# A state-space and gated-MLP block on one core: the recurrence tile laid out by residue, correction products written in contiguous runs, and a new order of stages

## The chip, the core and the metric

The kernel runs on one NeuronCore of a Trainium2 chip. The metric is the time of one execution on the device in microseconds (us); lower is better. The profile's span, first to last instruction, is 2 to 3 us shorter than this time (351.6 of 353.73 us before). TensorE is called PE in the profile, its weight load PEld, VectorE DVE, ScalarE ACT, GpSimd POOL, and SP issues the DMAs. "Busy" is the time in which something of an engine, or of a group of instructions, was running. Where one instruction follows another on an engine, the two overlap in the trace (products before: 1.42 us long, 1.13 from start to start); "busy" counts such time once, while the mean duration of one instruction contains it in full. So busy times of groups that alternate cannot be added, and for cost I use the distance from start to start and say so.

## The reference

```
x = A_x                                   # 2048 tokens x 640, bf16
xn = layernorm(x)
# A: a diagonal complex recurrence with 640 states
h[t] = Lam_bar * h[t-1] + (B_bar @ xn[t])
yA   = 2 * Re(C @ h[t]) + Dskip * xn[t]
# B: a gated MLP with mixing over tokens
z  = gelu(xn @ w_in);  z1 = z[:, :864];  z2 = layernorm(z[:, 864:])
g  = w_sp @ z2 + b_sp                     # 2048 x 2048 times 2048 x 864
yB = (z1 * g) @ w_out
out = x + yA + yB
```

## The kernel before

A small scheduler inside the kernel lists all operations with guessed costs, simulates the engines and fixes one order of instructions for each queue. TensorE's order is the program's own. All queues then run strictly in that order, and a wait at the head holds up what stands behind it (in the DMA queue once for 17.4 us, as shown below).

Time is split into 256 blocks of eight tokens; the token of residue j is the j-th of its block. The recurrence is done in three parts: inside each block (`horner`, seven steps from residue to residue), over the 256 block ends (`scan`), and a correction that adds the block's incoming state to each residue (`fix`). The tile of states keeps four residues interleaved, so that one residue is a row of 2-byte elements four apart:

```python
def lj(q, j):                 # q: which 128 of the 640 states
    return lv(q, j // 4).rearrange("p (x j) -> p x j", j=4)[:, :, j % 4]

def horner(q, j, half):       # 70 steps of 3; (r, m) = (re/im, 128 blocks)
    ...
    scalar_tensor_tensor(tv, prev, lr, cur, mult, add)                    # L648, 256 wide, float32 out
    scalar_tensor_tensor(dst[:, 0], prev[:, 1], nli, tv[:, 0], mult, add) # L650, 128 wide, bf16 out
    scalar_tensor_tensor(dst[:, 1], prev[:, 0], li,  tv[:, 1], mult, add) # L652, 128 wide, bf16 out

def fix(q, jg):
    pv = [m.ap(2048).rearrange("p (r n j) -> p r n j", r=2, j=4) for m in (P, Q)]
    for jj in range(n):       # n = 4 or 3 residues
        activation(pv[0][:, :, :, jj], hv[:, 1:3, 1:257], Identity, scale=a)  # L707, planned at ca(512, ptr=1) = 0.615 us
        activation(pv[1][:, :, :, jj], hv[:, 0:2, 1:257], Identity, scale=b)  # L709
    lq += P;  lq += Q         # L713, 2048 wide, all four residues at once
# an output tile of residue j waits for l_iv(q, j // 4): all four residues of its group

z2_tiles(0, 8)
for q in range(5):            # state inputs and recurrence, first half of the tokens
    bu(q, 0, 0); bu(q, 1, 0); horner(q, 1..7, 0)
z2_tiles(8, 16)
... kappa(); t_comb(0, 2, 4, 6)          # sums of z2 for the spatial product (L853)
for q in range(5):            # the same for the second half, then the scan
    bu(q, 0, 1); bu(q, 1, 1); horner(q, 1..7, 1); scan(q)
... z1 tiles, stored to DRAM; c_scaled()
for j in range(8): s_comb(j); spatial(j); ...   # 7 products instead of 8; sums of W on VectorE (L874)
outputs
```

## Time and profile before

| | before |
|---|---|
| time, median | 354.48 us (352.74 to 355.24, 3 runs); 354.86 us with a fourth |
| profiled span | 351.6 us |
| TensorE busy / waiting | 290.2 us / 58.2 us (sum of the waits below) |
| mean granted clock | 0.913 |
| VectorE, ScalarE busy | 247.8 us, 207.4 us |

The page's second part shows 40 slices of 8.8 us; a digit is the busy share in tenths, PEclk the granted clock.

```profile
PE   7799999999999505999896563497397699999996
...
DVE  4868999999999999999894542355655333345442
ACT  2899999964545201236979999999999221000000
...
PEclk9899999999999955999999686678879699999999
```

Slices are counted from 0. VectorE is full from slice 4 to 18 (35 to 167 us; the scans end at 158), ScalarE from slice 21 to 30 (185 to 272 us), and TensorE has holes beside both. Only the last quarter is TensorE's alone.

What TensorE waited for, in total, by the waits:

```profile
PE ps L917 <- ACT arena L930: 28.9, 9, 5.6
PE ps L917 <- ACT arena L602: 16.3, 1, 16.3
PE ps L999 <- DVE arena L1016: 8.3, 2, 5.5
PE ps L532 <- DVE arena L518: 3.0, 1, 3.0
PE ps L463 <- POOL arena L459: 1.3, 1, 1.3
PE ps L917 <- DVE arena L874: 0.4, 1, 0.4
```

The columns are total us, number and longest. The spatial products (L917) waited 28.9 us for evictions on ScalarE (L930) and once 16.3 us for z1's gelu (L602), which itself waited for a store. Groups of instructions, shapes kept apart (busy us, mean ns of one, then idle time before):

```profile
L707 ACT ACTIVATE arena<-arena 128x512 bf16<-128x512 bf16 x35 | 49.7, 1421 | 1.5 <-DVE arena L839 1.0 <-DVE arena L713 0.3
L709 ACT ACTIVATE arena<-arena 128x512 bf16<-128x512 bf16 x35 | 49.4, 1412 | 0.1
L648 DVE SCALAR_TENSOR_TENSOR arena<-arena 128x256 f32<-128x256 bf16 x70 | 31.4, 478 | 0.3
L650 DVE SCALAR_TENSOR_TENSOR arena<-arena 128x128 bf16<-128x128 bf16 x60 | 27.0, 508 | 0.0
L713 DVE TENSOR_TENSOR arena<-arena 128x2048 bf16<-128x2048 bf16 x20 | 24.5, 1224 | 41.0 <-ACT arena L707 28.2 <-ACT arena L709 12.8
```

A product (L707, L709) lasts 1.4 us for 512 elements, while the squares of 864 contiguous elements on the same engine (L573) last 0.94 us. The DMA queue's timeline before the 16.3 us pause (start, us issuing, what):

```profile
98.95 14.19 SPq L353 DMA_DIRECT2D z_scratch<-arena  x12
130.51 1.24 SPq L351 DMA_TRANSPOSE arena<-in_B_w_sp_dram  x1
131.80 1.05 SPq L353 DMA_DIRECT2D z_scratch<-arena  x2
```

From 113 to 130.5 us nothing is issued: a load of W stands at the head, and two stores of z1 behind it.

### The profile page before, as it was taken

The numbers are of one execution on the slowest core, as the hardware profiler recorded it, in microseconds if no ns is written. First come the engines' busy times: TensorE is split into PE (matmuls) and PEld (weight loads), VectorE is DVE, ScalarE is ACT, GpSimd is POOL, SyncE is SP. The second block draws the span as 40 slices with busy tenths as digits, with TensorE's granted clock in tenths as the row PEclk, the third lists the DMA queues.
The fourth block names the chain that finished last, engine by engine and source line by source line (L and its number), as shares of the span: only waits on it lengthen the run. The fifth ranks groups of instructions, "written<-read, shape, count | busy, mean of one in ns | idle before, by whom it ended". The sixth has DMA issues, their size and how long they took to land.

```text
span 351.6 us, 4404 instructions
## 1 busy us (share of the span) xinstructions
PE 290.2 (83%) x1587; PEld 169.8 (48%) x1587; DVE 247.8 (70%) x611; ACT 207.4 (59%) x270; POOL 26.7 (8%) x50
## 2 busy tenths in 40 slices
PE   7799999999999505999896563497397699999996
PEld 3454445544777402545443221154144357777774
DVE  4868999999999999999894542355655333345442
ACT  2899999964545201236979999999999221000000
POOL 3439320011000000000000000000000000000000
PEclk9899999999999955999999686678879699999999
DMA  7968463000054008577969391057422030552211
GB/s 245 229 145 220 90 89 62 2 0 0 2 171 150 3 0 241 120 147 122 191 132 209 95 202 37 0 106 111 103 66 74 23 82 2 108 129 75 76 56 37
DMA packets 81186, 34.73 MB, mean 99 GB/s; under 512 B 68526, under 2 KB 81166, under 8 KB 81166
## 3 DMA queue, kind: packets, MB, share of 16 engines
q1 hardware_dynamic: 81022, 34.39, 43.1%
q8 instruction: 12, 0.20, 0.2%
q14 instruction: 8, 0.07, 0.1%
q10 hardware_dynamic: 144, 0.08, 0.1%
HBM read 12.29 MB, written 6.18 MB: 53 GB/s over the span
## 4 chain that ended last, share of the span: by engine, by line
DVE 36%; PE 30%; ACT 28%; POOL 3%; issue 2%; DVEq 0%; POOLq 0%
ACT arena L707 12%; ACT arena L709 12%; PE ps L999 11%; DVE arena L648 7%; DVE arena L650 7%; PE ps L917 7%; PE ps L1007 7%; DVE arena L652 6%; DVE arena L668 4%; PE ps L559 3%; DVE arena L853 2%; POOL arena L749 2%; PE ps L463 2%; DVE arena L590 1%; ACT arena L930 1%
## 5 line engine op out<-in xcount | busy, mean ns | idle before, releaser
L917 PE MATMUL ps<-arena 128*128 128x432 bf16 x448 | 96.6, 381 | 45.6 <-ACT arena L930 28.9
L917 PEld LDWEIGHTS ps<-arena 128*128 128x128 bf16 x448 | 46.5, 106 | 94.8 <-ACT arena L930 33.0
L559 PE MATMUL ps<-arena 128*128 128x432 bf16 x320 | 61.4, 351 | 0.0
L999 PE MATMUL ps<-arena 128*128 128x320 bf16 x320 | 51.0, 319 | 8.3 <-DVE arena L1016 8.3
L713 DVE TENSOR_TENSOR arena<-arena 128x2048 bf16<-128x2048 bf16 x20 | 24.5, 1224 | 41.0 <-ACT arena L707 28.2
L707 ACT ACTIVATE arena<-arena 128x512 bf16<-128x512 bf16 x35 | 49.7, 1421 | 1.5 <-DVE arena L839 1.0
L709 ACT ACTIVATE arena<-arena 128x512 bf16<-128x512 bf16 x35 | 49.4, 1412 | 0.1
L559 PEld LDWEIGHTS ps<-arena 128*128 128x128 bf16 x320 | 38.7, 122 | 19.0 <-issue 1.5
L999 PEld LDWEIGHTS ps<-arena 128*128 128x128 bf16 x320 | 37.6, 118 | 20.3 <-DVE arena L1016 9.0
L617 PE MATMUL ps<-arena 128*128 128x512 bf16 x200 | 45.3, 386 | 0.0
L930 ACT ACTIVATE arena<-ps,arena 128x432 f32<-128x432 f32 (+1 forms) x32 | 19.7, 618 | 28.1 <-PE ps L917 28.1
L1007 PE MATMUL ps<-arena 128*128 128x320 bf16 (+1 forms) x224 | 33.1, 299 | 0.0
L602 ACT ACTIVATE arena<-ps 128x864 bf16<-128x864 f32 x16 | 14.0, 891 | 30.4 <-DMA z_scratch<-arena 21.6
L648 DVE SCALAR_TENSOR_TENSOR arena<-arena 128x256 f32<-128x256 bf16 x70 | 31.4, 478 | 0.3
L617 PEld LDWEIGHTS ps<-arena 128*128 128x128 bf16 x200 | 19.2, 96 | 25.7
L650 DVE SCALAR_TENSOR_TENSOR arena<-arena 128x128 bf16<-128x128 bf16 (+1 forms) x70 | 29.9, 485 | 0.0
L652 DVE SCALAR_TENSOR_TENSOR arena<-arena 128x128 bf16<-128x128 bf16 (+1 forms) x70 | 29.6, 483 | 0.2
L1016 DVE TENSOR_TENSOR arena<-ps,arena 128x640 bf16<-128x640 f32 x15 | 12.3, 823 | 23.3 <-PE ps L1007 23.3
L1007 PEld LDWEIGHTS ps<-arena 128*128 128x128 bf16 (+1 forms) x224 | 21.9, 98 | 8.3
L623 ACT CAST arena<-ps 128x1024 bf16<-128x1024 f32 x20 | 20.1, 1014 | 9.8 <-PE ps L617 9.6
L874 DVE TENSOR_TENSOR arena<-arena 128x1024 bf16<-128x1024 bf16 x32 | 22.1, 692 | 1.6 <-PE ps L917 1.6
L668 DVE TENSOR_TENSOR arena<-arena 128x512 f32<-128x512 f32 (+2 forms) x40 | 22.2, 577 | 0.0
(87 smaller groups left out, 251.1 us busy)
## 6 DMA issues: line engine op xcount, KB each, us to landing
arena<-in_A_x_dram SPq DMA_DIRECT2D x32, 160.0 KB, 3.2
z_scratch<-arena SPq DMA_DIRECT2D x16, 216.0 KB, 2.0
arena<-z_scratch SPq DMA_DIRECT2D x8, 432.0 KB, 4.7
out_dram<-arena SPq DMA_DIRECT2D x15, 160.0 KB, 2.0
arena<-in_B_w_in_dram SPq DMA_DIRECT2D x10, 216.0 KB, 3.9
arena<-in_B_w_out_dram SPq DMA_DIRECT2D x1, 960.0 KB, 6.3
arena<-in_B_w_sp_dram SPq DMA_TRANSPOSE x32, 4.0
arena<-arena SPq DMA_TRANSPOSE x20, 2.9
```

What stands on the lines that cost most here:

```text
L559: r = e.matmul(ps[:, b + h, 0:FG], lhs(k), winv[:, k, hcol * FH + h * FG:hcol * FH + (h + 1) * FG], start=(k == 0), stop=(k == ND - 1))
L617: r = e.matmul(ps[:, b + ri, :], btv[:, ri, k, q * 128:(q + 1) * 128], rhs[k], start=(k == 0), stop=(k == ND - 1))
L648: dve(lambda e: e.scalar_tensor_tensor(tv, prev, lr, cur, op0=ALU.mult, op1=ALU.add), rd + cr, [t.iv()], cd(256), nm + "a")
L650: dve(lambda e: e.scalar_tensor_tensor(dst[:, 0], prev[:, 1], nli, tv[:, 0], op0=ALU.mult, op1=ALU.add), rd + cr + [t.iv(0, 512)], dw[0:1] ...
L652: dve(lambda e: e.scalar_tensor_tensor(dst[:, 1], prev[:, 0], li, tv[:, 1], op0=ALU.mult, op1=ALU.add), rd + cr + [t.iv(512, 512)], dw[1:2 ...
L668: tt = lambda o, a, b, op: (lambda e: e.tensor_tensor(o, a, b, op))
L707: act(lambda e, a=a, jj=jj: e.activation(pv[0][:, :, :, jj], hv[:, 1:3, 1:257], ACT.Identity, scale=a), [h.iv(), Civ("a")], [P.iv()], ca(5 ...
L709: act(lambda e, b=b, jj=jj: e.activation(pv[1][:, :, :, jj], hv[:, 0:2, 1:257], ACT.Identity, scale=b), [h.iv(), Civ("b")], [Q.iv()], ca(5 ...
L713: dve(lambda e, m=m: e.tensor_tensor(lq, lq, m.ap(2048), ALU.add), [l_iv(q, jg), m.iv()], [l_iv(q, jg)], cd(2048, 2), "fix%s%d%d" % (nm, q ...
L917: r = e.matmul(ps[:, bk, 0:FG], lv_[:, k, :], rv[k], start=(first and k == 0), stop=(k == 7), skip_group_check=True)
L999: r = e.matmul(ps[:, b + n, 0:320], hv[:, o:o + 128], cpv[:, ri, q, n * 320:(n + 1) * 320], start=(q == 0 and ri == 0), stop=False, skip_g ...
L1007: r = e.matmul(ps[:, b + n, 0:320], gv[0:kk, k, :], wov[0:kk, k, n * 320:(n + 1) * 320], start=False, stop=(k == 6), skip_group_check=True)
```

## The change

The intent is that every write of 2-byte elements be contiguous. The state tile becomes residue-major, so a recurrence step takes all 256 blocks at once in half as many instructions; the copies from PSUM take the residues apart; products get small contiguous tiles of their own; corrections are done residue by residue, just ahead of the outputs. Around that: all z2 tiles come first, loads and warm-up at the start are reordered, fewer layernorm tiles go to ScalarE, and a pointer scalar costs 0.06 us more in the plan. (Gate products 864 wide, sums of W on VectorE and the output base from strided rows of x stand in both kernels; the diff does not touch them.)

```diff
 def lj(q, j):
-    return lv(q, j // 4).rearrange("p (x j) -> p x j", j=4)[:, :, j % 4]
+    return l_m.ap(512, BF16, (q * 8 + j) * 1024)
 # bu: state inputs out of PSUM
-act(lambda e: e.copy(o, ps[:, b:b + 2, :]), ...)                     # 1024 wide
+for ri in range(2):
+    act(lambda e, ri=ri: e.copy(o[:, ri, :, half, :], ps[:, b + ri, :].rearrange("p (m j) -> p j m", j=4)), ...)
 # horner: the same three instructions, 512, 256 and 256 wide, once per (q, j); two q interleaved
-def horner(q, j, half):
+def horner(q, j):
 # fix
-def fix(q, jg):   # 4 residues, products interleaved, 2 adds of 2048
+def fix(j):       # all five q of one residue
+    for q in range(5):
+        for lo, sc in ((1, a), (0, b)):
+            pv = m.ap(512).rearrange("p (r n) -> p r n", r=2)        # m: ring of 8 contiguous tiles
+            activation(pv, hv[:, lo:lo + 2, 1:257], Identity, scale=sc)
+            tensor_tensor(lq, lq, m.ap(512), add)
+                                                                 # (cut: residue 7, one copy for each q)
 # outputs
-pe(mmh, [l_iv(q, j // 4) for q in range(5)] + ...)
+pe(mmh, [l_iv(q, j) for q in range(5)] + ...)
 # order of stages
-z2_tiles(0, 8); <bu, horner of half 0>; z2_tiles(8, 16); <bu, horner of half 1, scan>
+z2 tiles 0..15, each before the next transpose; then per q: bu (both halves), t_comb, horner of two q, scan
+# start: loads "x0 w0 x1 w1 w2 x2 w3 w4 x3 x4 x5", gelu table loaded at once, 11 warm-up matmuls for 14
-ACT_LN = (3, 5, 7, 9, 11, 13, 15)
+ACT_LN = (3, 6, 9, 12)
+PTR = 0.06        # added to planned costs of instructions with a pointer scalar
 ... (sines grouped under one table load, scaled C computed in place)
```

More of the change, by code (lines that the diff above doesn't have):

```diff
@@ L279, in bass_parallel_sum__ssm_conv_s5__mixer_gmlp__prompt_kernel @@
         rt = r2.sub(14336)
-        ht_m = [rt.sub(1024) for _ in range(4)]
+        ht_m = [rt.sub(2048) for _ in range(2)]
         sc_m = [rt.sub(2048) for _ in range(3)]
-        s8_m = [rt.sub(2048) for _ in range(2)] + s_m[3:6]
-        e3 = Mem(wa_m.lo, 16384 + 3 * 2048)
+        s8_m = [rt.sub(2048) for _ in range(2)] + s_m[5:6]
+        e3 = Mem(wa_m.lo, 16384 + 5 * 2048)
         x_m = [e3.sub(1280) for _ in range(11)]
@@ L290, in bass_parallel_sum__ssm_conv_s5__mixer_gmlp__prompt_kernel @@
         q1 = r1.again()
-        pq_m = [q1.sub(4096) for _ in range(2)]
+        pq_m = [q1.sub(1024) for _ in range(8)]
         cf_m = [q1.sub(1728) for _ in range(5)]
@@ L375, in win_iv, with l_iv @@
             return win_m.iv((k * 2 + h) * FH * 2, FH * 2)
-        def l_iv(q, jg, ri=None, half=None):
+        def l_iv(q, j, ri=None, half=None):
+            o = (q * 8 + j) * 1024
             if ri is None:
-                return l_m.iv((q * 2 + jg) * 4096, 4096)
-            return l_m.iv((((q * 2 + jg) * 2 + ri) * 2 + half) * 1024, 1024)
-        def lv(q, jg):
-            return l_m.ap(2048, BF16, (q * 2 + jg) * 4096)
+                return l_m.iv(o, 1024)
+            return l_m.iv(o + ri * 512 + half * 256, 256)
         def lj(q, j):
-            return lv(q, j // 4).rearrange("p (x j) -> p x j", j=4)[:, :, j % 4]
+            return l_m.ap(512, BF16, (q * 8 + j) * 1024)
         cpos = {}
@@ L434, in bass_parallel_sum__ssm_conv_s5__mixer_gmlp__prompt_kernel @@
         FIRST = []
-        load_x(0, bias=5000)
-        load_win(0, 1, "sp", bias=4900)
-        load_x(1, bias=4800)
-        for k in range(1, ND):
-            load_win(k, 1, "sp", bias=4800 - 10 * k)
-        for i in range(2, 6):
-            load_x(i, bias=4700 - 10 * i)
+        for n, w in enumerate("x0 w0 x1 w1 w2 x2 w3 w4 x3 x4 x5".split()):
+            if w[0] == "x":
+                load_x(int(w[1]), bias=5000 - 20 * n)
+            else:
+                load_win(int(w[1]), 1, "sp", bias=5000 - 20 * n)
         for n, a in enumerate((A_Lambda_re, A_Lambda_im, A_log_dt)):
@@ L460, in bass_parallel_sum__ssm_conv_s5__mixer_gmlp__prompt_kernel @@
         pool(lambda e: e.memset(C("e"), math.e), [], [Civ("e")], 0.2, "e")
-        NW = 14
+        act(lambda e: e.activation(zero_m.ap(8, BF16, 1024), zero_m.ap(8), ACT.Gelu_apprx_tanh), [zero_m.iv(0, 1024)],
+            [zero_m.iv(1024, 16)], 1.4, "gelu table", bias=9000)
+        NW = 11
         for n in range(NW):
@@ L518, in ln_x @@
             dve(lambda e: e.tensor_scalar(xn.ap(D), x, mu, rstd, op0=ALU.subtract, op1=ALU.mult),
-                [xm.iv(), ri, mi if i in ACT_LN else siv(i, 12, 13)], [xn.iv()], cd(D, 4), "xn%d" % i)
+                [xm.iv(), ri, mi if i in ACT_LN else siv(i, 12, 13)], [xn.iv()], cd(D, 4) + 2 * PTR, "xn%d" % i)
         def xn_T(i):
@@ L591, in z2_norm @@
                                                         op0=ALU.subtract, op1=ALU.mult),
-                    [z2iv(i), s2iv(2, i, i + 1), s2iv(6, i, i + 1)], [z2iv(i)], cd(FH, 4), "z2n%d" % i)
+                    [z2iv(i), s2iv(2, i, i + 1), s2iv(6, i, i + 1)], [z2iv(i)], cd(FH, 4) + 2 * PTR, "z2n%d" % i)
         nz1 = [0]
@@ L621, in bu @@
                "bu%d%d%d" % (q, jg, half))
-            o = lv(q, jg).rearrange("p (r h x) -> p r h x", r=2, h=2)[:, :, half, :]
-            act(lambda e: e.copy(o, ps[:, b:b + 2, :]), [bank(b), bank(b + 1)],
-                [l_iv(q, jg, 0, half), l_iv(q, jg, 1, half)], ca(1024, psum=True), "u%d%d%d" % (q, jg, half))
+            o = l_m.ap(2048, BF16, (q * 8 + jg * 4) * 1024).rearrange("p (j r h m) -> p r j h m", j=4, r=2, h=2)
+            for ri in range(2):
+                act(lambda e, ri=ri: e.copy(o[:, ri, :, half, :], ps[:, b + ri, :].rearrange("p (m j) -> p j m", j=4)),
+                    [bank(b + ri)], [l_iv(q, jg * 4 + j, ri, half) for j in range(4)], ca(512, psum=True),
+                    "u%d%d%d%d" % (q, jg, half, ri))
@@ L626, in bass_parallel_sum__ssm_conv_s5__mixer_gmlp__prompt_kernel @@
         nh = [0]
         s8 = {}
-        def horner(q, j, half):
-            def part(ap):
-                return ap.rearrange("p (r h m) -> p r h m", r=2, h=2)[:, :, half, :]
-            prev, cur = part(lj(q, j - 1)), part(lj(q, j))
-            t = ht_m[nh[0] % 4]
+        def horner(q, j):
+            prev, cur = lj(q, j - 1), lj(q, j)
+            t = ht_m[nh[0] % 2]
             nh[0] += 1
-            tv = t.ap(256, FP32).rearrange("p (r m) -> p r m", r=2)
+            tv = t.ap(512, FP32)
@@ L636, in horner @@
             if j == 7:
-                d = s8_m[q]
+                d = s8_m[q % len(s8_m)]
                 s8[q] = d
-                dst = part(d.ap(512, FP32))
-                dw = [d.iv(ri * 1024 + half * 512, 512) for ri in range(2)]
+                dst = d.ap(512, FP32)
+                dw = [d.iv(0, 1024), d.iv(1024, 1024)]
             else:
                 dst = cur
-                dw = [l_iv(q, j // 4, ri, half) for ri in range(2)]
-            rd = [l_iv(q, jg, ri, half) for ri in range(2) for jg in {(j - 1) // 4, j // 4}]
+                dw = [l_m.iv((q * 8 + j) * 1024 + ri * 512, 512) for ri in range(2)]
@@ L645, in horner @@
+            pr = [l_m.iv((q * 8 + j - 1) * 1024 + ri * 512, 512) for ri in range(2)]
             lr, li, nli = C("a")[:, q:q + 1], C("b")[:, q:q + 1], C("nb")[:, q:q + 1]
             cr = [Civ("a"), Civ("b"), Civ("nb")]
-            nm = "h%d%d%d" % (half, q, j)
+            nm = "h%d%d" % (q, j)
             dve(lambda e: e.scalar_tensor_tensor(tv, prev, lr, cur, op0=ALU.mult, op1=ALU.add),
-                rd + cr, [t.iv()], cd(256), nm + "a")
-            dve(lambda e: e.scalar_tensor_tensor(dst[:, 0], prev[:, 1], nli, tv[:, 0], op0=ALU.mult, op1=ALU.add),
-                rd + cr + [t.iv(0, 512)], dw[0:1], cd(128), nm + "b")
@@ L652, in horner @@
-            dve(lambda e: e.scalar_tensor_tensor(dst[:, 1], prev[:, 0], li, tv[:, 1], op0=ALU.mult, op1=ALU.add),
-                rd + cr + [t.iv(512, 512)], dw[1:2], cd(128), nm + "c")
+                pr + [l_iv(q, j)] + cr, [t.iv()], cd(512) + PTR, nm + "a")
+            dve(lambda e: e.scalar_tensor_tensor(dst[:, 0:256], prev[:, 256:512], nli, tv[:, 0:256],
+                                                 op0=ALU.mult, op1=ALU.add),
+                pr[1:2] + cr + [t.iv(0, 1024)], dw[0:1], cd(256) + PTR, nm + "b")
@@ L656, in cs @@
+            dve(lambda e: e.scalar_tensor_tensor(dst[:, 256:512], prev[:, 0:256], li, tv[:, 256:512],
+                                                 op0=ALU.mult, op1=ALU.add),
+                pr[0:1] + cr + [t.iv(1024, 1024)], dw[1:2], cd(256) + PTR, nm + "c")
         def cs(m, q):
@@ L696, in hs_zero @@
                      [h.iv(b * 516, 4) for b in range(3)], 0.2, "hz%d" % q)
-        def fix(q, jg):
-            h = hs_m[q]
-            hv = h.ap(3 * 258).rearrange("p (b n) -> p b n", b=3)
-            P, Q = pq_m
-            pv = [m.ap(2048).rearrange("p (r n j) -> p r n j", r=2, j=4) for m in (P, Q)]
-            n = 4 if jg == 0 else 3
-            for jj in range(n):
-                j = jg * 4 + jj
-                a, b = C("a")[:, j * 5 + q:j * 5 + q + 1], C("b")[:, j * 5 + q:j * 5 + q + 1]
-                act(lambda e, a=a, jj=jj: e.activation(pv[0][:, :, :, jj], hv[:, 1:3, 1:257], ACT.Identity, scale=a),
-                    [h.iv(), Civ("a")], [P.iv()], ca(512, ptr=1), "P%d%d" % (q, j))
-                act(lambda e, b=b, jj=jj: e.activation(pv[1][:, :, :, jj], hv[:, 0:2, 1:257], ACT.Identity, scale=b),
-                    [h.iv(), Civ("b")], [Q.iv()], ca(512, ptr=1), "Q%d%d" % (q, j))
-            lq = lv(q, jg)
-            for m, nm in ((P, "p"), (Q, "q")):
-                dve(lambda e, m=m: e.tensor_tensor(lq, lq, m.ap(2048), ALU.add), [l_iv(q, jg), m.iv()],
-                    [l_iv(q, jg)], cd(2048, 2), "fix%s%d%d" % (nm, q, jg))
-            if jg == 1:
-                o = lj(q, 7).rearrange("p (r n) -> p r n", r=2)
-                act(lambda e: e.activation(o, hv[:, 1:3, 2:258], ACT.Copy), [h.iv()], [l_iv(q, 1)], ca(512),
-                    "h7_%d" % q)
@@ new lines, in bass_parallel_sum__ssm_conv_s5__mixer_gmlp__prompt_kernel @@
+        npq = [0]
+        def fix(j):
+            for q in range(5):
+                h = hs_m[q]
+                hv = h.ap(3 * 258).rearrange("p (b n) -> p b n", b=3)
+                if j == 7:
+                    o = lj(q, 7).rearrange("p (r n) -> p r n", r=2)
+                    act(lambda e, o=o, hv=hv: e.activation(o, hv[:, 1:3, 2:258], ACT.Copy), [h.iv()], [l_iv(q, 7)],
+                        ca(512), "h7_%d" % q)
+                    continue
+                a, b = C("a")[:, j * 5 + q:j * 5 + q + 1], C("b")[:, j * 5 + q:j * 5 + q + 1]
+                lq, li = lj(q, j), [l_iv(q, j)]
+                for lo, sc, cn, nm in ((1, a, "a", "P"), (0, b, "b", "Q")):
+                    m = pq_m[npq[0] % len(pq_m)]
+                    npq[0] += 1
+                    pv = m.ap(512).rearrange("p (r n) -> p r n", r=2)
+                    act(lambda e, pv=pv, hv=hv, lo=lo, sc=sc: e.activation(pv, hv[:, lo:lo + 2, 1:257], ACT.Identity,
+                                                                           scale=sc),
+                        [h.iv(), Civ(cn)], [m.iv()], ca(512, ptr=1), "%s%d%d" % (nm, q, j))
+                    dve(lambda e, m=m, lq=lq: e.tensor_tensor(lq, lq, m.ap(512), ALU.add), li + [m.iv()],
+                        li, cd(512, 2), "fix%s%d%d" % (nm, q, j))
@@ L754, in s5_consts @@
             frac(C("an"), C("rn"), [Civ("an")], [Civ("rn")], 80, "an")
-            act(lambda e: e.activation(C("rn"), C("an"), ACT.Sin, scale=6.2831845), [Civ("an")], [Civ("rn")], 1.5,
-                "cs")
-            C("a", 40)
-            C("b", 40)
-            C("nb", 5)
-            dve(tt(C("a"), C("rn")[:, 0:40], C("rk"), ALU.mult), [Civ("rn"), Civ("rk")], [Civ("a")], 0.1, "la")
-            dve(tt(C("b"), C("rn")[:, 40:80], C("rk"), ALU.mult), [Civ("rn"), Civ("rk")], [Civ("b")], 0.1, "lb")
-            dve(lambda e: e.tensor_scalar(C("nb"), C("b")[:, 0:5], -1.0, None, op0=ALU.mult), [Civ("b")], [Civ("nb")],
-                0.07, "lnb")
         def frac(a, t, ai, ti, n, name):
@@ L782, in tables @@
                                                               op0=ALU.mult),
-                    [it.iv(), Civ("an")], [u_m.iv(q * 1024, 1024)], cd(256, 2), "tu%d" % q)
+                    [it.iv(), Civ("an")], [u_m.iv(q * 1024, 1024)], cd(256, 2) + PTR, "tu%d" % q)
             c, s_, u = cos_m.ap(1280, FP32), sin_m.ap(1280, FP32), u_m.ap(1280, FP32)
             dve(lambda e: e.tensor_scalar(c, u, RND, None, op0=ALU.add), [u_m.iv()], [cos_m.iv()], cd(1280, 2), "tr")
-            dve(lambda e: e.scalar_tensor_tensor(c, c, RND, u, op0=ALU.subtract, op1=ALU.subtract),
-                [cos_m.iv(), u_m.iv()], [cos_m.iv()], cd(1280), "tf")
@@ L788, in tables @@
-            act(lambda e: e.activation(s_, c, ACT.Sin, scale=-6.2831845), [cos_m.iv()], [sin_m.iv()], ca(1280), "tsin")
-            act(lambda e: e.activation(c, c, ACT.Sin, scale=3.1415925), [cos_m.iv()], [cos_m.iv()], ca(1280), "thalf")
-            act(lambda e: e.activation(c, c, ACT.Square, scale=math.sqrt(2.0)), [cos_m.iv()], [cos_m.iv()], ca(1280),
+            dve(lambda e: e.scalar_tensor_tensor(u, c, RND, u, op0=ALU.subtract, op1=ALU.subtract),
+                [cos_m.iv(), u_m.iv()], [u_m.iv()], cd(1280), "tf")
@@ L791, in tables, with sins @@
+            def sins(e):
+                e.activation(C("rn"), C("an"), ACT.Sin, scale=6.2831845)
+                e.activation(s_, u, ACT.Sin, scale=-6.2831845)
+                return e.activation(c, u, ACT.Sin, scale=3.1415925)
+            act(sins, [Civ("an"), u_m.iv()], [Civ("rn"), sin_m.iv(), cos_m.iv()], 1.3 + 0.2 + 2 * 1.34 + 1.3, "sins")
+            act(lambda e: e.activation(c, c, ACT.Square, scale=math.sqrt(2.0)), [cos_m.iv()], [cos_m.iv()], ca(1280) + 0.15,
                 "tsq")
-            act(lambda e: e.activation(c, c, ACT.Copy, scale=-1.0, bias=1.0), [cos_m.iv()], [cos_m.iv()], ca(1280),
+            act(lambda e: e.activation(c, c, ACT.Copy, scale=-1.0, bias=1.0), [cos_m.iv()], [cos_m.iv()], ca(1280) + 0.1,
@@ L793, in tables @@
                 "tcos")
+            tt = lambda o, a, b_, op: (lambda e: e.tensor_tensor(o, a, b_, op))
+            C("a", 40)
+            C("b", 40)
+            C("nb", 5)
+            dve(tt(C("a"), C("rn")[:, 0:40], C("rk"), ALU.mult), [Civ("rn"), Civ("rk")], [Civ("a")], 0.1, "la")
+            dve(tt(C("b"), C("rn")[:, 40:80], C("rk"), ALU.mult), [Civ("rn"), Civ("rk")], [Civ("b")], 0.1, "lb")
+            dve(lambda e: e.tensor_scalar(C("nb"), C("b")[:, 0:5], -1.0, None, op0=ALU.mult), [Civ("b")], [Civ("nb")],
+                0.07, "lnb")
@@ L833, in c_scaled @@
                     o = cpv[:, c, q, :]
-                    t = pq_m[0]
-                    tv = t.ap(D, FP32)
-                    act(lambda e, y=y, tv=tv, k2=k2: e.activation(tv, y.ap(D), ACT.Identity, scale=k2),
-                        [y.iv(), Civ("k")], [t.iv()], ca(D, ptr=1), "cy%d%d" % (q, c))
-                    dve(lambda e, o=o, x=x, tv=tv, k1=k1, op=op: e.scalar_tensor_tensor(
-                            o, x.ap(D), k1, tv, op0=ALU.mult, op1=op, reverse1=(op == ALU.subtract)),
-                        [x.iv(), t.iv(), Civ("k")], [cp_m.iv((c * 5 + q) * 1280, 1280)], cd(D), "cp%d%d" % (q, c))
+                    oi = cp_m.iv((c * 5 + q) * 1280, 1280)
+                    act(lambda e, y=y, o=o, k2=k2: e.activation(o, y.ap(D), ACT.Identity, scale=k2),
+                        [y.iv(), Civ("k")], [oi], ca(D, ptr=1), "cy%d%d" % (q, c))
+                    dve(lambda e, o=o, x=x, k1=k1, op=op: e.scalar_tensor_tensor(
+                            o, x.ap(D), k1, o, op0=ALU.mult, op1=op, reverse1=(op == ALU.subtract)),
+                        [x.iv(), oi, Civ("k")], [oi], cd(D) + PTR, "cp%d%d" % (q, c))
         def t_comb(n):
@@ L984, in out_tile @@
                                           op1=ALU.mult),
-                [bsm.iv(), ms_m.iv()], [om.iv()], cd(D, 4), "xp%d%d" % (j, half))
+                [bsm.iv(), ms_m.iv()], [om.iv()], cd(D, 4) + 2 * PTR, "xp%d%d" % (j, half))
             dve(lambda e: e.tensor_tensor(om.ap(D), om.ap(D), dk_m.ap(D), ALU.mult), [om.iv(), dk_m.iv()],
@@ L1009, in mmg @@
                 return r
-            pe(mmh, [l_iv(q, j // 4) for q in range(5)] + [cp_m.iv()], [bank(b), bank(b + 1)], 20 * 0.136,
+            pe(mmh, [l_iv(q, j) for q in range(5)] + [cp_m.iv()], [bank(b), bank(b + 1)], 20 * 0.136,
                "oh%d%d" % (j, half))
@@ L1031, in bass_parallel_sum__ssm_conv_s5__mixer_gmlp__prompt_kernel @@
         xn_T(1)
-        def z2_tiles(t0, t1):
-            for i in range(t0, t1):
-                if i + 3 < NT:
-                    ln_x(i + 3)
-                if i + 2 < NT:
-                    xn_T(i + 2)
-                z2_tile(i)
-                if i == 2:
-                    load_bt(0)
-                    load_bt(1)
-                if i == 4:
-                    s5_consts()
-                if i < 5:
-                    load_x(i + 11)
-                if i % 4 == 3:
-                    z2_norm(i - 3, i + 1)
-        z2_tiles(0, 8)
-        tables()
-        hs_zero()
-        for q in range(5):
-            for jg in range(2):
-                bu(q, jg, 0)
-            for j in range(1, 8):
-                horner(q, j, 0)
-        z2_tiles(8, 16)
+        for i in range(NT):
+            if i + 3 < NT:
+                ln_x(i + 3)
+            z2_tile(i)
+            if i + 2 < NT:
+                xn_T(i + 2)
+            if i == 2:
+                load_bt(0)
+                load_bt(1)
+            if i == 4:
+                s5_consts()
+            if i == 6:
+                tables()
+                hs_zero()
+                kappa()
+            if i < 5:
+                load_x(i + 11)
+            if i % 4 == 3:
+                z2_norm(i - 3, i + 1)
         stats_turn()
@@ L1062, in bass_parallel_sum__ssm_conv_s5__mixer_gmlp__prompt_kernel @@
         dve(lambda e: e.tensor_copy(bsp_m.ap(16, FP32), bsb_m.ap(16)), [bsb_m.iv()], [bsp_m.iv()], 0.08, "bsp")
-        kappa()
-        for n in range(4):
-            t_comb(2 * n)
         for q in range(5):
             for jg in range(2):
-                bu(q, jg, 1)
+                for half in range(2):
+                    bu(q, jg, half)
+            if q < 4:
+                t_comb(2 * q)
             for j in range(1, 8):
-                horner(q, j, 1)
-            scan(q)
+                if q % 2 == 1 or q == 4:
+                    if q != 4:
+                        horner(q - 1, j)
+                    horner(q, j)
+            if q % 2 == 1 or q == 4:
+                if q != 4:
+                    scan(q - 1)
+                scan(q)
         for j in range(2):
@@ L1080, in bass_parallel_sum__ssm_conv_s5__mixer_gmlp__prompt_kernel @@
         c_scaled()
-        for q in range(5):
-            fix(q, 0)
-        for q in range(5):
-            fix(q, 1)
         outs = [(j, h) for j in range(8) for h in range(2)]
@@ L1090, in next_out @@
                 j, h = outs[no[0]]
+                if h == 0:
+                    fix(j)
                 no[0] += 1
```

## The prediction

> **What bounds the kernel now** (chain of waits, engine timelines; span 351.6 us).
> - 12 to 119 us: TensorE streams without a gap (z2, state inputs, z1); VectorE is full from 37 us with the recurrence.
> - 119 to 183 us: VectorE is still full (scans end at 158). Matmuls pause 16.3 us at 119 to 135. The waits name z1's gelu waiting for its store; the DMA queue's timeline shows the cause: it issued nothing from 113 to 130.5, as a load of W at its head waited for a sum of W, queued on VectorE behind the recurrence.
> - 183 to 275 us: ScalarE is busy 90 of 92 us with correction products (L707, L709); matmuls wait 28.9 us for evictions (L930) queued behind them; granted clock 0.81. From 275 us TensorE alone runs, 4.62 us an output tile.
> Matmuls wait some 58 us in all.
>
> **What the change does.**
> 1. Correction products: the same 70 of 512 elements, now contiguous. Starts are 1.13 us apart. Contiguous 640-wide activations start every 0.64 us; scaled to 512, with 0.09 for the pointer scale (L836 against L493), I estimate 0.62. ScalarE saves about 36 us, plus 3 on plain copies. [...]
> 2. Recurrence: 70 x 3 instructions (256, 128, 128 wide; starts 0.40 + 0.29 + 0.29) become 35 x 3 twice as wide: estimated 0.66 + 0.40 + 0.40. VectorE: 68.7 to 51 us, mostly from fewer instructions.
> 3. Copies from PSUM: 20 of 1024 (0.90) become 40 of 512 with strided reads (estimate 0.5 to 0.7): 2 to 10 us more, hidden under matmuls.
> 4. Correction adds: 20 of 2048 (1.15) become 70 of 512 (about 0.35): even.
> 5. All z2 tiles run first; the recurrence starts near 61 us instead of 38. VectorE idles meanwhile, which gives back most of the 17 us: scans end near 147 to 152, against 158.
> 6. Corrections go by residue, so an output needs ten products, not all seventy. The scheduler's costs now match the instructions (before, it planned 0.62 for 1.13, and 0.74 for a 0.98 step), so queue orders should hold and the 16.3 us pause should mostly go.
>
> **Critical path.** TensorE becomes the bound. From the trace: z2 to 45 us, state inputs to 91, z1 to 120, then eight spatial tiles of 10.2 and sixteen output tiles of 4.62, to 276, and 3 for the last store: floor 279. I add 10 us of stalls near 145 to 165, because the first gate transposes need the space of the scaled C, which waits for the scans, and 6 for half-speed clock after pauses ([...]the slices after the present pause show 0.5). Span 295, time 298.
>
> **Prediction: 298 us, 284 to 316. Faster by over 2% 0.95, within 2% 0.04, slower 0.01.**
>
> **Right or wrong by:** correction products starting 0.6 to 0.7 us apart; recurrence busy near 60 us; ScalarE total 155 to 170; matmul waits on evictions under 10 us; no long gap before the spatial matmuls; granted clock above 0.93; the chain mostly TensorE.
>
> **What would make it wrong:** strided PSUM reads at double cost; the 7.2 us POOL power stalling layernorm while z2 tiles run in a row; a VectorE chain that starts too late; DMA queue order still blocking z1 stores or gate transposes.

279 + 10 + 6 = 295 us, and 3 from span to time. The 6 was my estimate.

## The result and the profile after

| | before | after |
|---|---|---|
| time, median | 354.86 us | 285.73 us (284.39 to 286.86, 4 runs) |
| ratio (95% interval) | | 0.8059 (0.8006 to 0.8112) |
| profiled span | 351.6 us | 282.6 us |
| TensorE busy / waiting | 290.2 / 58.2 us | 270.0 / 9.4 us |
| granted clock | 0.913 | 0.993 |
| VectorE, ScalarE busy | 247.8, 207.4 us | 228.7, 158.4 us |

A ratio is the mean time of one kernel's fast runs over that of the other's in the same rounds, so it is not quite the ratio of the medians. The slices after:

```profile
PE   7799999999999999899999959989989999999995
...
DVE  4899845899999999899999998999999616354442
ACT  3799999985447554323323889999999300000000
...
PEclk9999999999999999999999979999999999999999
```

```profile
PE ps L923 <- ACT arena L936: 2.9, 1, 2.9
PE ps L532 <- DVE arena L518: 2.4, 3, 1.1
PE ps L1005 <- DVE arena L1022: 1.8, 2, 0.9
PE ps L463 <- POOL arena L457: 1.3, 1, 1.3
PE ps L923 <- ACT arena L602: 1.0, 1, 1.0
```

The sums close: before, 290.2 busy + 58.2 waiting + 3.2 other (the last store above all) = 351.6; after, 270.0 + 9.4 + 3.2 = 282.6. Of the 69.0 us, 48.8 are waits that went and 20.2 are TensorE busy time, although almost the same matmuls are done. The spatial matmuls account for 12.8 of the 20.2 (96.6 to 83.8 us) and the first part of the outputs for 4.9 (51.0 to 46.1). They are the matmuls that ran after pauses, at a lower granted clock: summed over the stretches that the kept traces record at half clock, TensorE was busy for 38.6 us before and 2.8 us after. Half of the difference, 17.9 us, is my estimate of what the clock cost: at half clock the 14 spatial matmuls recorded from 135.5 to 140.4 us took 0.35 us each, z1's, as wide, at full clock 0.18. The warm-up matmuls were busy another 1.4 us less (6.1 us for 14, 4.7 for 11). After the long pause, from 119.2 to 135.5 us, half clock was granted from 123.4 to 140.4 us, 5 us into the matmuls that follow. The only 7 after the change stands at a wait of 2.9 us: half clock was granted from 166.2 to 169.6 us, and eight matmuls took 2.8 us in it. So these two pauses were paid for twice. Groups that answer to those before:

```profile
L718 ACT ACTIVATE arena<-arena 128x512 bf16<-128x512 bf16 x70 | 44.4, 719 | 0.0
L721 DVE TENSOR_TENSOR arena<-arena 128x512 bf16<-128x512 bf16 x70 | 26.7, 415 | 1.0 <-ACT arena L718 1.0
L648 DVE SCALAR_TENSOR_TENSOR arena<-arena 128x512 f32<-128x512 bf16 x35 | 25.5, 745 | 0.0
L650 DVE SCALAR_TENSOR_TENSOR arena<-arena 128x256 bf16<-128x256 bf16 x30 | 14.1, 477 | 0.0
```

Start to start a product takes 0.61 us instead of 1.13, so 43 us for the 70 instead of 79. (The 49.7 and 49.4 us of L707 and L709 must not be added and set against 44.4: the two lines alternate and overlap each other.) A recurrence instruction of 256 bf16 elements (477 ns) is now shorter than one of 128 was (508 ns). The chain that ended last is TensorE for 91% (before: DVE 36%, PE 30%, ACT 28%):

```profile
PE 91%; DVE 3%; ACT 3%; DMA 1%; POOL 1%; issue 0%; SPq 0%; DVEq 0%
```

### The profile page after: what moved, and what is told of

It reads as the page before. It is cut to its first block, busy times and chain, and to the rows that moved or that the text cites. A ratio compares the mean times of both kernels' runs of the same rounds, so it can differ in the third digit from the quotient of the medians.

```text
span 282.6 us, 4366 instructions
## 1 busy us (share of the span) xinstructions
PE 270.0 (96%) x1584; PEld 159.7 (57%) x1584; DVE 228.7 (81%) x556; ACT 158.4 (56%) x278; POOL 26.1 (9%) x53
## 4 chain that ended last, share of the span: by engine, by line
PE 91%; DVE 3%; ACT 3%; DMA 1%; POOL 1%; issue 0%; SPq 0%; DVEq 0%
PE ps L923 28%; PE ps L559 19%; PE ps L617 16%; PE ps L1005 16%; PE ps L1013 11%; DMA arena<-in_A_x_dram 1%; PE ps L532 1%; ACT arena L718 1%; ACT arena L842 1%; DVE arena L505 1%; DVE arena L518 1%; DVE arena L1022 1%; DVE arena L506 1%; POOL arena L513 0%; ACT arena L936 0%
## 5 line engine op out<-in xcount | busy, mean ns | idle before, releaser
L923 PE MATMUL ps<-arena 128*128 128x432 bf16 x448 | 83.8, 350 | 3.9 <-ACT arena L936 2.9
L923 PEld LDWEIGHTS ps<-arena 128*128 128x128 bf16 x448 | 44.1, 99 | 43.1 <-ACT arena L936 3.3
L559 PE MATMUL ps<-arena 128*128 128x432 bf16 x320 | 60.4, 346 | 0.0
L559 PEld LDWEIGHTS ps<-arena 128*128 128x128 bf16 x320 | 38.2, 121 | 18.0
L1005 PE MATMUL ps<-arena 128*128 128x320 bf16 x320 | 46.1, 299 | 1.8 <-DVE arena L1022 1.8
L617 PE MATMUL ps<-arena 128*128 128x512 bf16 x200 | 45.2, 386 | 0.0
L718 ACT ACTIVATE arena<-arena 128x512 bf16<-128x512 bf16 x70 | 44.4, 719 | 0.0
L1005 PEld LDWEIGHTS ps<-arena 128*128 128x128 bf16 x320 | 31.1, 98 | 14.9 <-DVE arena L1022 2.5
L617 PEld LDWEIGHTS ps<-arena 128*128 128x128 bf16 x200 | 19.2, 96 | 25.8
L624 ACT CAST arena<-ps 128x512 bf16<-128x512 f32 x40 | 21.3, 593 | 13.2 <-PE ps L617 13.2
L721 DVE TENSOR_TENSOR arena<-arena 128x512 bf16<-128x512 bf16 x70 | 26.7, 415 | 1.0 <-ACT arena L718 1.0
L648 DVE SCALAR_TENSOR_TENSOR arena<-arena 128x512 f32<-128x512 bf16 x35 | 25.5, 745 | 0.0
L602 ACT ACTIVATE arena<-ps 128x864 bf16<-128x864 f32 x16 | 14.2, 890 | 13.5 <-PE ps L559 12.4
L670 DVE TENSOR_TENSOR arena<-arena 128x512 f32<-128x512 f32 (+2 forms) x40 | 21.4, 553 | 0.0
L653 DVE SCALAR_TENSOR_TENSOR arena<-arena 128x256 bf16<-128x256 bf16 (+1 forms) x35 | 16.6, 479 | 0.0
L650 DVE SCALAR_TENSOR_TENSOR arena<-arena 128x256 bf16<-128x256 bf16 (+1 forms) x35 | 16.5, 477 | 0.0
L573 ACT ACTIVATE arena<-arena 128x864 bf16<-128x864 bf16 x16 | 14.9, 937 | 0.0
```

Of the source, the lines that this page charges most:

```text
L559: r = e.matmul(ps[:, b + h, 0:FG], lhs(k), winv[:, k, hcol * FH + h * FG:hcol * FH + (h + 1) * FG], start=(k == 0), stop=(k == ND - 1))
L617: r = e.matmul(ps[:, b + ri, :], btv[:, ri, k, q * 128:(q + 1) * 128], rhs[k], start=(k == 0), stop=(k == ND - 1))
L624: act(lambda e, ri=ri: e.copy(o[:, ri, :, half, :], ps[:, b + ri, :].rearrange("p (m j) -> p j m", j=4)), [bank(b + ri)], [l_iv(q, jg * 4 ...
L648: dve(lambda e: e.scalar_tensor_tensor(tv, prev, lr, cur, op0=ALU.mult, op1=ALU.add), pr + [l_iv(q, j)] + cr, [t.iv()], cd(512) + PTR, nm ...
L670: tt = lambda o, a, b, op: (lambda e: e.tensor_tensor(o, a, b, op))
L718: act(lambda e, pv=pv, hv=hv, lo=lo, sc=sc: e.activation(pv, hv[:, lo:lo + 2, 1:257], ACT.Identity, scale=sc), [h.iv(), Civ(cn)], [m.iv()] ...
```

## Experiments

The question was which parts of the change carry the 69 us. My theory was that the products' writes bound one stage, VectorE's load another, and that release by residue and a truthful plan let TensorE run through. The rivals are in the expectations. Eleven of the twelve runs were fast (the state of a_probe, one execution, is unknown), and each is compared with the kernel before on its own chip.

| run | from | edit | median us | ratio (95%) |
|---|---|---|---|---|
| b_contig | before | products contiguous | 314.21 | 0.886 (0.882 to 0.890) |
| b_costs | before | true costs in the plan | 331.92 | 0.937 (0.934 to 0.941) |
| b_both | before | contiguous, true recurrence costs | 315.14 | 0.890 (0.885 to 0.894) |
| a_strided | after | products strided again | 321.59 | 0.908 (0.905 to 0.911) |
| a_group | after | release by groups of four | 299.06 | 0.844 (0.840 to 0.847) |
| a_halves | after | recurrence in two halves, contiguous | 298.01 | 0.841 (0.838 to 0.844) |
| a_lstrided | after | state tile interleaved again | 341.69 | 0.965 (0.961 to 0.968) |
| a_start | after | old start | 289.74 | 0.817 (0.815 to 0.820) |
| a_oldcost | after | PTR = 0 | 288.73 | 0.814 (0.811 to 0.817) |
| a_again | after | none | 285.3 | 0.804 (0.802 to 0.807) |
| a_v2 | after | two savings on TensorE | 282.01 | 0.797 (0.794 to 0.800) |
| a_probe | after | probes of write steps | one look | |

### b_contig: the products alone

```diff
-pv = [m.ap(2048).rearrange("p (r n j) -> p r n j", r=2, j=4) for m in (P, Q)]
+pv = [m.ap(2048).rearrange("p (j r n) -> p r n j", r=2, j=4) for m in (P, Q)]
```

> The kernel before with one edit: the correction products are written as contiguous runs of 256 into their tile, and the adds read the tile as they did, so the result is wrong on purpose while every instruction's count, size and order is the same. Theory (ScalarE writing 2-byte elements four apart bounds the stage from 183 to 275 us): products start about 0.62 us apart instead of 1.13, ScalarE busy falls by about 36 us in total, matmul waits on evictions fall from 28.9 us to under 8, and the time is 300 to 318 us. Rival (the gain comes from the order of the queues and from the wider recurrence, the writes are not slower): products stay near 1.1 us apart, time within 2% of 355.

It took 314.21 us, inside the range. Products lasted 0.71 us on average (0.61 start to start), ScalarE was busy 167.1 us instead of 207.4 (40 less), and the waits for evictions fell from 28.9 to 8.5 us, just over the 8 I had expected. The 16 us pause stayed (16.6 us). So one change of addresses, at the same count, size and order of instructions, is worth 40 us in the old kernel. The comparison with the reference at its tolerance does not see these products, so it is no proof of their layout.

### b_costs: the plan alone

```diff
-ca(512, ptr=1)  # products        -cd(256), cd(128), cd(128)  # recurrence step
+1.13                              +0.395, 0.29, 0.29
# also 1.13 for the copies to residue 7; no instruction changes
```

> The kernel before with the same instructions, but the scheduler is told what the trace shows: 1.13 us for a product, 0.395, 0.29 and 0.29 for the three instructions of a recurrence step. Only the queue orders change. Theory (the plan's wrong costs put a load of W ahead of z1's stores and caused the 16.3 us pause): the pause before the spatial matmuls shrinks to under 5 us; but ScalarE still has its 36 us too much after the scans, so the time falls only by 5 to 20 us, to 335 to 350. Rival (the order is the main thing): under 320 us.

331.92 us: below the theory's range and above the rival's, so neither had it right. The same instructions in another order are worth 22 us; most of it came at the evictions on ScalarE, whose waits fell from 28.9 to 15.9 us. And the part of the theory that named the cause of the pause fell: the pause stayed, with another name.

```profile
PE ps L917 <- DVE arena L853: 19.4, 2, 16.6
```

With the true costs no load of W stands ahead of z1's stores, but now the sums of z2 (L853) come late on VectorE, and the spatial products wait for them. My reading is that at 120 us VectorE had more to do than time for it, and that the plan only chose which piece came too late; the next run bears on this.

### b_both: do the two add up?

Edit: that of b_contig, with the planned costs of b_costs for the recurrence and the copies to residue 7.

> The kernel before with contiguous products (wrong on purpose, as in the run of that edit alone) and the true costs of the recurrence steps in the plan. Theory (the pause of about 16 us before the spatial matmuls is VectorE's load there, whatever the plan; the corrected plan had taken its 22 us from the stage that contiguous products already relieve): the pause stays at 10 to 20 us and the time is 300 to 312 us, so that another 15 to 25 us of the change come from the wider recurrence, the new stage order, the release by residue and the start. Rival (two independent gains add up): 292 us.

315.14 us: nothing beyond b_contig, and 3 us above my range. The waits for VectorE before and in the first spatial products came in pieces (9.7 us for L874, 3.9 for L853), and evictions still cost 7.3. In the traces of the kernel before, of b_contig and of b_both alike, TensorE has done 72 spatial matmuls by 151.4 us and then waits for a sum of W on VectorE (L874), although the first of them starts at 135.5, 135.3 and 120.5 us. So the queue order moved the pause, and VectorE set the time by which this stage was through. So the better plan and the faster products had relieved the same later stage, the evictions on ScalarE, and the 28 us from 314 to 286 come from the rest of the change.

### a_strided: the products undone in the new kernel

```diff
-pv = m.ap(512).rearrange("p (r n) -> p r n", r=2)
+pv = <slot k % 4 of an interleaved tile of four>          # elements four apart
-tensor_tensor(lq, lq, m.ap(512), add)
+tensor_tensor(lq, lq, lq, add)                            # wrong on purpose, same form and wait
```

> The kernel after with one part undone: the products are written four elements apart again (four products share an interleaved tile), and each add reads its own other operand twice in place of the product, so that VectorE's work keeps its form; wrong on purpose. Theory: products start about 1.13 us apart, ScalarE gets about 36 us more, and as it is full from 150 us on after the change, the outputs wait for it: 305 to 320 us. Rival (release by residue and the better plan carry the gain, ScalarE has slack): under 292 us.

321.59 us, 36 more than the kernel after, and 2 above my range; the rival is far off. ScalarE's products were busy 83.9 us instead of 44.4 (1413 ns each instead of 719), and TensorE waited 22.8 us for evictions. ScalarE's 39.5 us pass into the time almost whole: there is no slack for them behind the release by residue.

### a_group: release by residue undone

```diff
-if h == 0: fix(j)
+if h == 0 and j % 4 == 0: fix(j); fix(j + 1); fix(j + 2); fix(j + 3)
-pe(mmh, [l_iv(q, j) for q in range(5)] + ...)
+pe(mmh, [l_iv(q, jj) for q in range(5) for jj in <its group of four>] + ...)
```

> The kernel after with the release by residue undone: an output tile waits for the corrections of its whole group of four residues, as before. Theory: the first output now waits for 40 products (about 25 us of ScalarE besides the evictions) instead of ten, so TensorE stands 10 to 18 us at the first outputs and the time is 293 to 303 us. Rival (the spatial matmuls hide it): within 1% of 286.

299.06 us, as the theory had it. The first output's matmuls start at 193.5 us instead of 182.8, after waits of 3.0, 1.7, 3.8 and 4.5 us in the stretch from 164 to 193.5 us.

### a_halves: instruction count on VectorE

Edit: `horner(q, j)` calls the three instructions twice, on 128 blocks each, in the contiguous tile.

> The kernel after, contiguous layout kept, but each recurrence step again in two halves (70 x 3 instructions of 256, 128 and 128 elements instead of 35 x 3 of 512, 256 and 256). Theory (on VectorE the win is the fixed cost of 105 instructions, not the layout): recurrence 68 to 69 us of starts instead of 51, scans end some 12 to 17 us later, and since the scaled C and the first gate transposes wait for them, TensorE pauses 8 to 15 us: 293 to 302 us. Rival (layout is the win on VectorE too): recurrence under 60 us, time within 1% of 286.

298.01 us, in the theory's range. The group lines:

```profile
L655 DVE SCALAR_TENSOR_TENSOR arena<-arena 128x256 f32<-128x256 bf16 x70 | 30.4, 476 | 0.0
L657 DVE SCALAR_TENSOR_TENSOR arena<-arena 128x128 bf16<-128x128 bf16 x60 | 20.6, 344 | 0.0
```

Start to start the three are 0.395 + 0.263 + 0.263, so 70 steps take 64.5 us, not the 68 to 69 that I had written; the kernel after needs 51 (35 x 1.46), the kernel before 68.6 (70 x 0.98). So 4 us of VectorE's saving are layout at this width and 13.5 are fixed cost: 0.263 us for 128 elements and 0.395 for 256 leave, by my estimate, 0.13 for each instruction, and there are 105 fewer. The scans end at 168 us instead of 155, and TensorE waits 5.8 us for evictions and 7.0 us for sums of W that stand behind the recurrence.

### a_lstrided: the state tile undone

```diff
-return l_m.ap(512, BF16, (q * 8 + j) * 1024)
+return <tile of four residues>.rearrange("p (x j) -> p x j", j=4)[:, :, j % 4]
 # copies from PSUM, horner and fix use this view; width, count, order and waits unchanged
```

> The kernel after with only the layout of the recurrence tile undone: residues interleaved four apart again, at the new width and order; products stay contiguous in their own tiles. Correct result. Theory: the scalar_tensor_tensor steps cost almost the same (at most 0.03 us more each, 2 to 3 us in all); the adds [...]0.34 to about 0.62 us each, 20 us more VectorE but spread over a stage with slack; ScalarE's copies from PSUM are unchanged: 287 to 296 us. Rival (strided 2-byte writes cost VectorE what they cost ScalarE, nearly double): recurrence above 75 us, time above 305.

341.69 us: my expectation fell, by 46 us. Most of the change's gain is lost by this alone.

```profile
L722 DVE TENSOR_TENSOR arena<-arena 128x512 bf16<-128x512 bf16 x70 | 86.4, 1336 | 0.0
...
L649 DVE SCALAR_TENSOR_TENSOR arena<-arena 128x512 f32<-128x512 bf16 x35 | 25.2, 736 | 0.0
L651 DVE SCALAR_TENSOR_TENSOR arena<-arena 128x256 bf16<-128x256 bf16 x30 | 23.3, 791 | 0.0
```

```profile
PE ps L924 <- ACT arena L937: 27.0, 12, 7.4
PE ps L1006 <- DVE arena L1023: 22.8, 2, 14.6
```

An add lasts 1336 ns instead of 415; start to start it takes 1.10 us instead of 0.34, and I had expected 0.62 (adds of 512 float32 elements start 0.60 us apart in the kernel after). That is some 53 us more of VectorE for the 70 adds, against some 11 for the recurrence, and it falls in the stage of the outputs: TensorE waits 27.0 us for evictions on ScalarE and 22.8 us for evictions on VectorE. (The rival's time came true, its recurrence above 75 us did not: it needs about 62.) The step that reads strided but writes float32 in a row is unchanged (736 ns against 745): strided reads cost this instruction nothing. The add both reads and writes strided, and the two were not taken apart for it. The steps that write strided bf16 take 791 ns instead of 477, and start to start 0.58 us instead of 0.395, exactly twice the 0.29 us that 128 such elements took before. Nine adds in a row take 1.13 us each for 512. All are 2.1 to 2.3 ns per element, and so are ScalarE's old products (1.13 us for 512). At 128 elements this was hidden, because fixed cost and computing need 0.263 us anyway; I had read the small difference at 128 (0.29 against 0.263) as the price of the stride, when it was only the part that stuck out. Wider instructions paid only where the writes were contiguous: strided, one of 256 cost what two of 128 cost (0.58 us).

### a_probe: the price of a write by itself

Edit: at the start, four instructions of each form on each engine, 512 or fewer 2-byte elements read in a row.

> The kernel after with a row of probes at its start (correct result; only the probes' durations count): four copies on ScalarE and four scalar_tensor_tensor on VectorE of each form, from contiguous 2-byte input. Theory A (a 2-byte element written alone costs about 2.2 ns, whatever the step): 512 elements at steps 2, 4 and 8 all about 1.13 us apart on both engines, contiguous 0.53 on ScalarE and 0.61 to 0.66 on VectorE; runs of two 2-byte elements at step 4 as fast as contiguous; 4-byte elements at steps 2 and 4 as fast as contiguous; 128 elements at step 4 about 0.29. Theory B [...]: steps 2 and 4 at full rate, only step 8 slow. Theory C (any element written alone is slow, 4-byte too): 4-byte elements at steps 2 and 4 also near 1.1.

Some of the views; each line's next instruction gives the distance. ScalarE in a row, then step 2 (its first three; two narrow windows split what a wide one merges), then step 4 and step 8:

```profile
2.15 2.17 ACT L474 ACTIVATE arena<-arena 128x512 bf16<-128x512 bf16 x4
4.35 2.02 ACT L474 ACTIVATE arena<-arena 128x512 bf16<-128x512 bf16 x3
...
9.65 4.78 ACT L474 ACTIVATE arena<-arena 128x512 bf16<-128x512 bf16 x4
14.18 0.78 ACT L522 ACTIVATE arena<-arena 128x640 bf16<-128x640 bf16 x1
...
15.53 9.28 ACT L474 ACTIVATE arena<-arena 128x512 bf16<-128x512 bf16 x4
24.31 1.21 ACT L596 ACTIVATE arena<-ps 128x864 bf16<-128x864 f32 x1
```

VectorE, step 2 then step 4:

```profile
4.21 2.56 DVE L480 SCALAR_TENSOR_TENSOR arena<-arena 128x512 bf16<-128x512 bf16 x4
6.67 0.47 DVE L533 BATCH_NORM_STATS2 arena<-arena 128x6 f32<-128x320 bf16 x1
...
7.97 4.72 DVE L480 SCALAR_TENSOR_TENSOR arena<-arena 128x512 bf16<-128x512 bf16 x4
12.50 0.20 DVE L534 BATCH_NORM_AGGREGATE arena<-arena 128x2 f32<-128x12 f32 x1
```

For instance (14.18 - 9.65) / 4 = 1.13 us. In the same way, us for one instruction, start to start:

| written | ScalarE | VectorE |
|---|---|---|
| 512 of 2 bytes, in a row | 0.52 | 0.63 |
| 512 of 2 bytes, step 2 | 0.62 | 0.62 |
| 512 of 2 bytes, step 4 | 1.13 | 1.13 |
| 512 of 2 bytes, step 8 | 2.20 | 2.22 |
| 512 of 2 bytes, pairs, a pair every 4 elements | 0.52 | 0.59 |
| 512 of 4 bytes, in a row | 0.52 | 0.60 |
| 512 of 4 bytes, step 2 | 0.54 | 0.60 |
| 512 of 4 bytes, step 4 | 0.92 | 0.91 |
| 256 of 2 bytes, step 4 | 0.55 | 0.56 |
| 128 of 2 bytes, step 4 (in a row) | 0.27 (0.20) | 0.26 (0.20) |

(ScalarE ran the first two forms back to back, eight in 4.86 us; single instructions start 0.52 us apart in the first and 0.62 in the second. Where an idle stretch follows, its distance is left out. The probes of the two engines overlapped in part, in step 2 nearly whole; ScalarE's products alone show the same 1.13.) All three theories fell. The price is not one per lone element (A): step 2 costs VectorE nothing and ScalarE a fifth (0.62 against 0.52), far from 1.13, and step 8 costs twice step 4. Step 4 is not at full rate (B): 1.13 us against 0.52 and 0.63 in a row. And lone 4-byte elements at step 2 cost next to nothing (0.54 against 0.52 us, and 0.60 against 0.60), though at step 4 they are slow (C). As an estimate from these numbers: with lone 2-byte writes an instruction takes about 0.27 ns for each byte of the stretch over which it spreads them (1.13 us for 4 KB, 2.2 for 8, 0.55 for 2, 0.27 for 1), with lone 4-byte writes about 0.11 (0.92 us for 8 KB), or its own time, whichever is longer; pairs of 2-byte elements took no longer than a row (0.52 us and 0.59). ScalarE at step 2 does not quite fit: 2 KB would give 0.55 us, and it took 0.62. Other offsets were not tried, so this stays an estimate.

### a_start and a_oldcost: the small parts

Edits: the old load order, 14 warm-up matmuls, no early table load and seven layernorm tiles on ScalarE; and `PTR = 0.0`.

> The kernel after with the start undone: old order of the first loads, 14 warm-up matmuls, gelu table loaded on demand, seven layernorm tiles on ScalarE instead of four. Theory: the first z2 matmul begins near 11.6 us instead of 7.6, and a TensorE-bound kernel passes that on: 3 to 6 us, 289 to 292 us. Rival (the start is absorbed later): within 1 us of the kernel after.

> The kernel after with the scheduler's new surcharge of 0.06 us per pointer scalar set to zero; instructions are the same, only queue orders may change. Theory (orders hold because costs are near the truth; 0.06 matters on VectorE's full stretch): 286 to 296 us, with pauses of TensorE of up to 10 us more. Rival (no effect): within 1% of 286.

The start: 289.74 us, 4 us, as expected in size but not in mechanism. The first z2 matmul begins at 8.5 us against 7.6, not at 11.6; the rest came as longer waits later (4.9 us at an eviction instead of 2.9, 0.9 for a DMA transpose). Before, it began at 11.6, and the trace shows a third transpose waiting 3.0 us ahead of it; the new loop puts the tile before that transpose, which this run left in place. The surcharge: 288.73 us, about 1% above the kernel after, inside the range of both expectations, so this run does not tell them apart; small and, across two chips, not settled.

### a_v2: a faster version

TensorE bounds the kernel after (270.0 of 282.6 us busy, 91% of the chain), so I looked for less TensorE work. The state inputs' moving operand took four tokens of every eight; since ScalarE's copies from PSUM separate residues anyway, the matmul can take 512 tokens in a row. Three more transposes go to the DMA.

```diff
-rhs = [xnTv[:, k, half*1024:(half+1)*1024].rearrange("p (m j) -> p m j", j=8)[:, :, jg*4:jg*4+4] for k in range(ND)]
+rhs = [xnTv[:, k, c*512:(c+1)*512] for k in range(ND)]            # c = jg * 2 + half
-e.copy(o[:, ri, :, half, :], ps[:, b + ri, :].rearrange("p (m j) -> p j m", j=4))
+e.copy(o[:, ri, c, :, :],    ps[:, b + ri, :].rearrange("p (m j) -> p j m", j=8))
-DMA_T = (9, 11, 13, 15)
+DMA_T = (9, 10, 11, 12, 13, 14, 15)
```

> An attempt to beat the kernel after, which TensorE bounds: the state inputs are multiplied over 512 tokens in a row (the residues are taken apart by the copy from PSUM instead of by the matmul's moving operand), and three more xn tiles are turned by the DMA instead of by TensorE. Theory: 200 state-input matmuls go from 0.226 to about 0.216 us apart, 2.0 us, and three transposes of 0.28 us go, 0.8 us: 282 to 284.5 us, ratio to before about 0.798. Rival (the stride costs TensorE nothing, or later DMA transposes stall z2): no gain, or slower.

> The kernel after itself, for a comparison on the same chip: 285 to 287 us, ratio 0.806 as before.

282.01 against 285.3 us on the same chip, ratios 0.797 and 0.804 with intervals that do not touch, result correct. The two savings were not run singly; the matmuls below account for 1.8 of the 3 us. TensorE's timelines, the kernel after and then this one:

```profile
41.64 45.17 PE L617 MATMUL ps<-arena 128*128 128x512 bf16 x200
```

```profile
40.86 43.33 PE L617 MATMUL ps<-arena 128*128 128x512 bf16 x200
```

200 matmuls of 512 columns take 43.3 us, 0.217 each, instead of 45.2, 0.226. z1's 160 matmuls of 432 columns, whose moving operand is contiguous too, take 29.36 us in both, which scaled by columns is 0.217 for 512: as an estimate, the whole price of the stride is gone. ScalarE's copies, now in runs of 64, last the same (591 ns against 593).

## Why the prediction was right

The measured 285.73 us lies in the range of 284 to 316, near its lower end, and the direction was right; 298 was 12 us too high.

- **The bounds of the stages** held, and b_contig shows the third of them directly.
- **Step 1, products 0.62 us:** measured 0.61. a_strided shows the worth: 36 us in the time.
- **Step 2, recurrence 0.66 + 0.40 + 0.40:** measured the same, 58.6 us of busy time against "near 60". "Mostly from fewer instructions" is right as arithmetic (13.5 of 17.5 us) but misses the condition: with strided writes the wider instructions would have gained little (a_lstrided).
- **Steps 3 and 4:** copies from PSUM 0.48 us each, adds 0.34 us start to start. The strided PSUM reads cost nothing to speak of: a_lstrided reads PSUM in a row, and its copies take 0.48 us too.
- **Step 5:** the recurrence starts at 57 us (61 predicted) and the scans end at 155 (147 to 152). But VectorE does not merely idle before it: seven of the sixteen sums of z2 are done from 52 to 59 us and the last at 96, in time for the spatial products at 117 (before: 84 to 141 us).
- **Step 6, two errors.** The first outputs before waited for the forty products of their group of four, not for all seventy; a_group puts the worth at 13 us. And the 16.3 us pause was put down to queue order. b_costs corrected the plan and kept the pause. So, with b_both, what shortened it should be less and earlier VectorE work; a_halves, which adds VectorE work alone, gives part of it back (7.0 us of waits for sums of W). Which of the new stage order and the shorter recurrence did more was not separated.
- **The size.** The predicted 10 us of stalls at 145 to 165 measured 2.9, and instead of 6 us the half clock cost about 1.4 (2.8 us of matmuls ran at it; granted 0.993). The start gave 4 us that I had not counted (z2 ended at 41.6 instead of 45). These three come to about 15 us, against the 12 by which the number was too high.

Undone singly in the new kernel, the layout of the state tile costs 56 us, and products, release, instruction count and start cost 36, 13, 12 and 4 us. They are not to be summed (together they exceed the 69 us of the whole change), for two of them can relieve the same wait, as b_costs, b_contig and b_both show.

## What to carry to other kernels

Look at the addresses that an instruction writes before its width: on both engines 2-byte writes four apart cost 2.2 ns an element, about twice the time of contiguous ones (1.13 us against 0.52 and 0.63 for 512), and small instructions hide this under their fixed cost until they are widened (128 elements 0.29 us against 0.263, 256 elements 0.58 against 0.395). Where one side has to be strided, let it be the read: strided reads cost the recurrence on VectorE (736 ns strided, 745 in a row) and the copies on ScalarE (593 ns in both) nothing here, TensorE's moving operand 4% (0.226 us against 0.217, a_v2). A wait names the piece that came last; when a corrected order only gives the pause a new name, as here, suspect that the engine behind it is overloaded and that work has to be removed or moved to where that engine has time. And a pause of TensorE can be paid for again in clock (0.35 us a matmul instead of 0.18 after the long pause): of 69 us won here, by my estimate about 18 were the same matmuls running faster.
